# Notes on one change to an attention and squared-ReLU kernel: the first batch, the small first weights and two blocks of plain products

## The chip, the cores and the metric

The kernel runs on one core of one Trainium2 chip. The metric is the device time of one execution, in microseconds (us), as the median of several runs. The engines are TensorE (PE in the profile), VectorE (DVE), ScalarE (ACT), GpSimd (POOL) and SyncE (SP), which here only issues DMA transfers. Each engine takes its instructions in the order of the program; between engines they wait on semaphores.

## The reference

```python
def mab(q, kv):
    s = scale * (q @ kv.transpose(0, 2, 1))
    s = s - s.max(-1, keepdims=True)
    a = np.exp(s)
    a /= a.sum(-1, keepdims=True) + 1e-09
    return a @ kv
h = mab(I, x)            # I: inducing, (32, 128); x: (4, 12480, 128)
y = mab(x, h)            # (4, 12480, 128)
u = np.maximum(y.reshape(49920, 128) @ w_in, 0.0)    # w_in: (128, 2048)
out = u * u @ w_out                                  # w_out: (2048, 128)
```

For each of the four batches, 32 inducing rows attend to the 12480 rows of x (first attention) and give h, 32 rows. Then each row of x attends to these 32 rows (second attention), and its result goes through a feed-forward layer with a squared ReLU. The weights come as 64-bit floats.

## The kernel before, in words

**Blocks and groups.** The rows of a batch are cut into 26 lanes of 480 rows; four lanes are a group (the seventh group has two). A lane is also a block of the feed-forward part: 104 blocks. The second attention's weights for a lane, `st` (128x480, the 32 weights four times below each other, as high and low parts), are multiplied with `hw` = h @ w_in. So for each block PE makes 16 products `h` (L769), ACT takes the ReLU (L776) and the square (L790), DVE splits the squares into a high part (`hi`, L795) and a low part (`lo`, L800), and PE multiplies these with the split w_out: hi by wo_hi, hi by wo_lo, lo by wo_hi (L835), 45 products, and one of the 16 pieces in fp32 with `wo_whole` (L825), which PE does in two passes. The result bank `op` is turned by DVE (L855) and stored (L861).

**The first attention of batch 0** (class `First`, `early`): for each group in turn the rows `xn` come in one transfer (L407), PE turns them by transposes (L445) into `xtp`, ACT and DVE copy these out to `xt` (L242), PE makes the scores `sp` (L503), and then the group finds its maximum over rows and lanes (`mx`, `lanes`, `gather`, `most`, `neg`: L510 to L528), takes the exponentials `e` with that shift (L538), turns them to `et` (L548), mixes them with the rows (`nb`, L556), and adds that to what the groups so far gave, rescaled by `fade` (L566, L572). `first_end` then makes `zp`, `htp`, `hT` and, with w_in, the four pieces `wp` of `hw` (L623 to L632). The later batches' first attention runs between the blocks of the batch before, with rows turned on DVE: `xb` comes in 8 small transfers (L477) into the only such buffer, and DVE turns it (L480).

**Weights.** Each of the 8 pieces of w_in (i0 to i3) and w_out (o0 to o3) is loaded as words (L341, L353), sized on ACT and rebuilt on DVE in five steps, and joined; pieces of w_out are then split. The pieces share the buffers `hi` and `lo`, two each, with the blocks.

**Second attention** (class `Second`): scores `na` (L665), turned on DVE, maximum, difference, exponential on ACT, sum, normalised, turned back, split into `sw`, and spread by DMA to `st` (L713; 4 transfers for a lane, on SP's queue). For block 0 there is a small one of its own (`mini`, names with m: `na_0m`, `d_0m`, `sw_0m`), of four pieces of 128 rows, spread by 16 transfers on ACT's queue.

**What sets the order.** Nothing is issued as it is written. Each piece of work is a `Task` with an engine, a length, a due time and needs, and `Plan.run` places them one after another by these lengths and due times; in the order of that plan the instructions are then written out. The needs and due times set only the order on each engine. What an instruction waits for on the chip is its data and its buffers.

## Time and profile before

| | us |
|---|---|
| median of 3 runs | 1669.66 (1668.59 to 1670.12) |
| the profiled execution, own time | 1670.68 |
| its span | 1668.8 |
| PE busy in the span | 1617.4 (97%) |
| DVE busy | 1561.5 (94%) |
| ACT busy | 1522.7 (91%) |
| first `h` of block 0 starts | 81.44 |
| output turns of block 0, block 1 start | 111.50, 126.97 |

Rows of a timeline read: start, length, engine, line, operation, out<-in, shapes, count, and in brackets the engine's idle time ahead of it and what ended it. SPq and ACTq are the queues' issues of transfers. Rows of busy time by stretch read: stretch, its length, then PE, PEld, DVE, ACT and POOL busy with their counts, the clock granted to PE (1.00 is full), the busy share of the DMA engines, and GB/s. Rows of groups end with total busy time, mean ns of one, and idle time ahead.

### The profile page before, as it was taken

The numbers are of one execution on the slowest core, as the hardware profiler recorded it, in microseconds if no ns is written. First come the engines' busy times: TensorE is split into PE (matmuls) and PEld (weight loads), VectorE is DVE, ScalarE is ACT, GpSimd is POOL, SyncE is SP. The second block draws the span as 40 slices with busy tenths as digits, with TensorE's granted clock in tenths as the row PEclk, the third lists the DMA queues.
The fourth block names the chain that finished last, engine by engine and source line by source line (L and its number), as shares of the span: only waits on it lengthen the run. The fifth ranks groups of instructions, "written<-read, shape, count | busy, mean of one in ns | idle before, by whom it ended". The sixth has DMA issues, their size and how long they took to land.

```text
span 1668.8 us, 22357 instructions
## 1 busy us (share of the span) xinstructions
PE 1617.4 (97%) x8042; PEld 1289.8 (77%) x8042; DVE 1561.5 (94%) x1524; ACT 1522.7 (91%) x1444; POOL 49.0 (3%) x38
## 2 busy tenths in 40 slices
PE   7489999999999999999999999989999999999998
PEld 4168788887777888888877888877887788778886
DVE  7689999999999999999999999989999999989997
ACT  4289999999999999999989999989999999999997
POOL 0000000000001000000000000000000000000000
PEclk9689999999999999999999999999999999999999
DMA  7334333223243431334124433132111121111111
GB/s 248 84 68 94 64 75 81 41 55 72 47 89 60 86 79 31 74 53 88 30 58 93 82 59 78 36 66 54 24 30 40 39 42 36 36 35 35 21 28 20
DMA packets 389855, 101.57 MB, mean 61 GB/s; under 512 B 369232, under 2 KB 385904, under 8 KB 389744
## 3 DMA queue, kind: packets, MB, share of 16 engines
q1 hardware_dynamic: 388976, 99.89, 28.7%
q8 instruction: 64, 1.05, 0.3%
q14 instruction: 47, 0.39, 0.1%
q10 hardware_dynamic: 768, 0.25, 0.1%
HBM read 48.94 MB, written 25.56 MB: 45 GB/s over the span
## 4 chain that ended last, share of the span: by engine, by line
PE 91%; DVE 3%; DMA 2%; SPq 1%; ACT 1%; issue 1%; ACTq 0%; DVEq 0%
PE op L835 59%; PE h L769 21%; PE op L825 5%; PE na L665 1%; PE nb L556 1%; PE sp L503 1%; PE wp L623 1%; DVE lo L800 1%; SPq L477 1%; DMA st<-sw 0%; PE xtp L445 0%; ACT g L776 0%; ACT g L790 0%; DVE hi L795 0%; SPq L713 0%
## 5 line engine op out<-in xcount | busy, mean ns | idle before, releaser
L776 ACT ACTIVATE g<-h 128x960 f32<-128x960 f32 x832 | 781.2, 983 | 80.6 <-PE h L769 48.3
L800 DVE TENSOR_TENSOR lo<-g,hi 128x1920 fp32r<-128x1920 f32 (+2 forms) x419 | 839.9, 2005 | 12.6
L790 ACT ACTIVATE g<-g 128x1920 f32<-128x1920 f32 (+1 forms) x419 | 760.3, 1814 | 4.3
L769 PE MATMUL h<-st,hw 128*128 128x480 f32 x1664 | 510.9, 389 | 19.6 <-DMA xb<-in_x_dram 15.2
L795 DVE CAST hi<-g 128x1920 fp32r<-128x1920 f32 (+2 forms) x419 | 451.9, 1079 | 38.8 <-ACT g L790 33.9
L835 PE MATMUL op<-hi,wo_hi 128*128 128x480 f32 x1560 | 454.8, 405 | 0.5 <-DVE hi L795 0.4
L835 PE MATMUL op<-hi,wo_lo 128*128 128x480 f32 x1560 | 442.1, 382 | 0.0
L835 PE MATMUL op<-lo,wo_hi 128*128 128x480 f32 x1560 | 425.1, 382 | 6.4 <-DVE lo L800 6.4
L769 PEld LDWEIGHTS h<-st,hw 128*128 128x128 f32 x1664 | 310.7, 189 | 105.2 <-issue 38.0
L835 PEld LDWEIGHTS op<-hi,wo_hi 128*128 128x128 f32 x1560 | 293.1, 189 | 83.6 <-issue 37.4
L835 PEld LDWEIGHTS op<-lo,wo_hi 128*128 128x128 f32 x1560 | 291.5, 188 | 60.7 <-DVE lo L800 9.0
L835 PEld LDWEIGHTS op<-hi,wo_lo 128*128 128x128 f32 x1560 | 293.1, 188 | 49.2 <-issue 2.6
L825 PE MATMUL op<-g,wo_whole 128*128 128x480 f32 x208 | 100.5, 564 | 0.0
L690 POOL TENSOR_SCALAR z<-z 128x15 f32<-128x15 f32 (+1 forms) x28 | 47.9, 1711 | 1516.7 <-DVE z L686 1462.8
L855 DVE STREAM_TRANSPOSE ob<-op 128x480 f32<-128x480 f32 (+1 forms) x105 | 70.4, 671 | 4.1 <-PE op L835 3.9
L480 DVE STREAM_TRANSPOSE xt<-xb 128x960 f32<-128x960 f32 x39 | 45.3, 1163 | 7.5 <-DMA xb<-in_x_dram 5.3
L825 PEld LDWEIGHTS op<-g,wo_whole 128*128 128x128 f32 x208 | 38.9, 188 | 5.9
L556 PE MATMUL nb<-xn,et 128*32 128x128 f32 (+1 forms) x840 | 30.8, 280 | 5.8 <-DVE et L548 5.7
L556 PEld LDWEIGHTS nb<-xn,et 128*32 128x32 f32 (+1 forms) x840 | 23.5, 111 | 16.5 <-DVE et L548 9.4
L503 PE MATMUL sp<-xt,indT 128*32 128x480 f32 x208 | 31.2, 594 | 4.2 <-DVE xt L242 2.7
L242 ACT COPY xt<-xtp 128x256 f32<-128x256 f32 (+1 forms) x33 | 11.1, 366 | 21.1 <-PE xtp L445 17.9
L665 PE MATMUL na<-xt,hT 128*32 128x480 f32 (+1 forms) x224 | 27.5, 568 | 0.0
(103 smaller groups left out, 423.0 us busy)
## 6 DMA issues: line engine op xcount, KB each, us to landing
out_dram<-ob SPq DMA_DIRECT2D x412, 60.0 KB, 2.2
xn<-in_x_dram SPq DMA_DIRECT2D x24, 960.0 KB, 5.5
st<-sw SPq DMA_DIRECT2D x380, 60.0 KB, 2.0
xb<-in_x_dram SPq DMA_DIRECT2D x312, 60.0 KB, 2.6
xn<-in_x_dram SPq DMA_DIRECT2D x4, 480.0 KB, 4.9
hi_i<-in_moe_w_in_dram SPq DMA_DIRECT2D x2, 512.0 KB, 10.4
lo_i<-in_moe_w_in_dram SPq DMA_DIRECT2D x2, 512.0 KB, 8.5
hi_o<-in_moe_w_out_dram SPq DMA_DIRECT2D x2, 512.0 KB, 7.6
```

The lines of the kernel that those rows point to most:

```text
L480: nc.vector.transpose(self.xt_tile(h).rearrange("c l r t -> c (l r t)"), v["xb"].rearrange("p l r c -> p (l r c)"))
L503: nc.tensor.matmul(v["sp"][q * M:(q + 1) * M, :LANE], indT, s["xt"][self.g, q // 2][:, q % 2].rearrange("c r t -> c (r t)"), start=True, s ...
L556: nc.tensor.matmul(v["nb"][c * M:(c + 1) * M, :], self.et[:R, r, :], self.xn[:R, r, :], start=r < Q, stop=r >= NR - Q,)
L690: E.tensor_scalar(v["z"], v["z"], 1e-9, 0.0, ALU.add, ALU.add)
L769: nc.tensor.matmul(c["hp"][:, l, :LANE], s["hw"][:, f * P:(f + 1) * P], second.st[k], start=True, stop=True,)
L776: nc.scalar.activation(v["g"][:, 2 * i:2 * i + 2, :], c["hp"][:, :, :LANE], AF.Relu)
L790: nc.scalar.activation(v["g"][:, h], v["g"][:, h], AF.Square)
L795: nc.vector.tensor_copy(v["hi"][:, h], v["g"][:, h])
L800: nc.vector.tensor_sub(v["lo"][:, h], v["g"][:, h], v["hi"][:, h])
L825: nc.tensor.matmul(w["op"][:, :LANE], wo_whole, v["g"][:, 3, :], start=False, stop=False)
L835: nc.tensor.matmul(w["op"][:, :LANE], wo[:, 4 * j + l, :], v[name][:, l, :], start=(j == x_ == 0 and l == 0), stop=(j == NQ - 1 and x_ == ...
L855: nc.vector.transpose(w["ob"][:, rows].rearrange("p r c -> p (r c)"), w["op"][:, rows.start * S:rows.stop * S])
```

## The change

**First batch.** A class `FirstBatch` takes the place of seven early `First`. All groups are turned and scored first; the scores stay (groups 0 to 3 are copied to `sk` in `st` buffers, the last three stay in their PSUM banks), each group's maximum goes to a column of `bare`, and one maximum over all of them gives one `neg`. Then come seven exponentials, and all mixes accumulate in the one bank `nb`; there is no rescaling. Transposes fill two banks at once, so that an eviction is 8 or 7 row blocks of all four lanes (up to 1024 columns). x loads stand ahead of most weight loads on SP's queue. PSUM is given out anew when `hT` is done (`open_g`).

**Small first weights.** `mini` now takes four pieces that lie next to each other; DVE writes high and low parts side by side (`sk`), four PE products with an identity turn and repeat them into one bank (`ap`), and ACT and DVE copy that bank to `st`. The 16 transfers are gone.

**Blocks 0 and 1** (`PLAIN`): the squares are not split; 16 products with the joined fp32 pieces `whole` of w_out make a block. The pieces' split to wo_hi and wo_lo is done later, before block 2.

**Order.** Due times and lengths in the plan are changed (`T_MAIN`, `ORDER`, `W_DUE`, transfers, products); some tasks have added needs (`GATES`, `begun`, "spread", "products", "h"), which act on the order only. `xt` is one tile for each group instead of two.

```diff
-    GB, HB, LB, OB, MB, STB, XTB, XNB, XBB = 3, 2, 2, 2, 2, 6, 14, 2, 1
-    T_MAIN, BLOCK = 44100.0, 15100.0
-    ORDER = "x0 x1 i0 x2 i1 x3 i2 x4 i3 x5 x6 o0 o1 o2 o3".split()
-    W_DUE = [11900.0, 21000.0, 24900.0, 30200.0, 40500.0, 46000.0, 50000.0, 53300.0]
-    SPARE = (3, 5, 6)
-    FIRST_DUE, FIRST_STEP = 6000.0, 4300.0
+    GB, HB, LB, OB, MB, STB, XTB, XNB, XBB = 3, 2, 2, 2, 2, 6, 7, 2, 1
+    T_MAIN, BLOCK = 42100.0, 15100.0
+    ORDER = "x0 x1 x2 x3 i0 x4 x5 x6 i1 i2 i3 o0 o1 o2 o3".split()
+    W_DUE = [11900.0, 21100.0, 24900.0, 30200.0, 41500.0, 46000.0, 50000.0, 53300.0]
+    FIRST_DUE, FIRST_STEP, MIX_DUE, MIX_STEP, MINI_DUE = 6000.0, 2600.0, 25000.0, -1000.0, -800.0
     S2_LEAD, S2_LEAD_0, S2_STEP, S1_LEAD, S1_STEP = 44500.0, 26000.0, 1600.0, 11100.0, 3000.0
     WHOLE = lambda b, g, k: True
+    PLAIN = lambda b, g, k: b == g == 0 and k < 2
+    GATES = lambda s, m: dict(
+        s0=m.ready[0], s1=m.ready[0], s2=m.ready[0], s3=m.ready[0], w0_1=m.normed, w0_2=m.normed, w0_3=m.normed,
+        o1=m.normed, o2=m.normed, o3=m.normed,
+    )
+    SPLIT_DUE, SPLIT_STEP, PLAIN_DUE = 64000.0, 0.0, 9500.0
...
+    ps_t = early_scope.enter_context(tc.tile_pool(name="ps_t", bufs=2, space=PSUM))
+    ps_s = early_scope.enter_context(tc.tile_pool(name="ps_s", bufs=4, space=PSUM))
+    plan = Plan(dict(xn=XNB, early=5, tp=2, s=4, xb=XBB, xt=XTB, st=STB, m=MB, h=2, o=OB, g=GB, hi=HB, lo=LB, sw=1, a=1, d=2, e=2, et=2), T_MAIN, patience=PATIENCE)
...
-        pools["early_scope"].close()
+        early_scope.close()
+        pools["h"] = ctx.enter_context(tc.tile_pool(name="ps_h", bufs=2, space=PSUM))
+        pools["o"] = ctx.enter_context(tc.tile_pool(name="ps_o", bufs=OB, space=PSUM))
+        pools["m"] = ctx.enter_context(tc.tile_pool(name="ps_m", bufs=MB, space=PSUM))
+        wo_pool = ctx.enter_context(tc.tile_pool(name="wo", bufs=1, side="right"))
+        pools["wo"] = [wo_pool.tile([P, NF, C], F32R, name=f"wo_{part}") for part in ("hi", "lo")]
         pools["g"] = ctx.enter_context(tc.tile_pool(name="g", bufs=GB, side="right"))

...
             def use(v, needs, due, kw, k=k):
-                hi = wo_hi[:, k * m:(k + 1) * m, :].rearrange("p f c -> p (f c)")
-                lo = wo_lo[:, k * m:(k + 1) * m, :].rearrange("p f c -> p (f c)")
+                def part(i):
+                    return pools["wo"][i][:, k * m:(k + 1) * m, :].rearrange("p f c -> p (f c)")
+
+                def join():
+                    v["whole"] = v["a"].bitcast(F32)
+                    nc.vector.tensor_add(v["whole"], v["whole"], v["b"])
+
+                def keep():
+                    nc.scalar.copy(wo_whole, v["whole"][:, (m - 1) * C:m * C])

                 def split():
-                    nc.scalar.copy(hi, v["a"].bitcast(F32))
+                    nc.scalar.copy(part(0), v["whole"])

                 def rest():
-                    a = v["a"].bitcast(F32)
-                    on(tr).tensor_sub(a, a, hi)
-
-                def join():
-                    on(tj).tensor_add(lo, v["a"].bitcast(F32), v["b"])
-
-                def whole():
-                    c = slice((m - 1) * C, m * C)
-                    nc.vector.tensor_add(wo_whole, v["a"][:, c].bitcast(F32), v["b"][:, c])
-
-                t = add("ACT", 530, split, due, needs, **kw)
+                    nc.vector.tensor_sub(part(1), v["whole"], part(0))
+
+                t = add("DVE", 600, join, due, needs, port=True, **kw)
                 if k == n - 1:
-                    t = add("DVE", 200, whole, due, [t] + needs, port=True, **kw)
-                tr = add("DVE", length("DVE"), rest, due, [t], port=True, **kw)
-                tj = add("DVE", length("DVE"), join, due, [tr], port=True, **kw)
-                return tj
+                    w_kept.append(add("ACT", 280, keep, SPLIT_DUE, [t], **kw))
+                d = SPLIT_DUE + k * SPLIT_STEP
+                th = w_gate[f"s{k}"] = add("ACT", 530, split, d, [t], **kw)
+                tl = add("DVE", 600, rest, d, [th], port=True, **kw)
...
+    class FirstBatch:
...
+            t = add("DVE", 100, lanes, d - 3000, self.tops)
+            t = add("DVE", 110, lanes2, d - 3000, [t])
+            t = add("PE", 110, gather, d - 3000, [t], reads=[bg])
+            t = add("DVE", 100, most, d - 3000, [t], reads=[bg])
+            shifted = add("DVE", 70, shift, d - 3000, [t])
...
+            powered, mixed = None, None
+            for g in range(NG):
+                R = M * lanes_of[g]
+                c = {}
+                be, bet = Buffer("e"), Buffer("et")
+
+                def power(g=g, R=R, c=c):
+                    c["e"] = att.tile([P, NR, S], F32, tag="e", name=f"e_0_{g}")
+                    nc.scalar.activation(
+                        c["e"][:R].rearrange("p r t -> p (r t)"), self.sp[g], AF.Exp,
+                        bias=self.neg[:R], scale=scale, accum_out=bare[:R, 1, g:g + 1],
+                    )
...
+                def mix(g=g, R=R, c=c):
+                    if g == 0:
+                        v["nb"] = early_bank("nb_0")[:, :C]
+                    for r in range(NR):
+                        k = r % Q
+                        nc.tensor.matmul(
+                            v["nb"][k * M:(k + 1) * M, :], c["et"][:R, r, :], self.xn[g][:R, r, :],
+                            start=g == 0 and r < Q, stop=g == NG - 1 and r >= NR - Q,
+                        )
...
+                bank_ = Buffer("tp")
+                v = {}
+
+                def turn(rs=rs, v=v):
+                    v["tp"] = ps_t.tile([P, 8, P], F32, tag="tp", name=f"xtp_0_{g}_{rs.start}")
+                    for j, r in enumerate(rs):
+                        nc.tensor.transpose(v["tp"][:, j, :R], self.xn[g][:R, r, :], ident[:R, :R])
+
+                def turned(rs=rs, v=v):
+                    if rs.start == 0:
+                        s["xt"][g] = xt_pool.tile([C, Q, NR, S], F32, tag="xt", name=f"xt_0_{g}")
+                    copy(
+                        v["task"], s["xt"][g][:, :L, rs.start:rs.stop, :].rearrange("c l r t -> c r l t"),
+                        v["tp"][:, :len(rs), :R].rearrange("c r (l t) -> c r l t", l=L),
+                    )
+
+                t = state["turn"] = add(
+                    "PE", 109 * len(rs), turn, due + 300 * k / 4, [self.loaded[-1], state.get("turn")], mode="t",
+                    takes=[bank_], reads=[self.bxs[g]],
+                )
+                n = R * len(rs)
+                v["task"] = add("ACT|DVE", (wide_ns(n, "ACT"), wide_ns(n)), turned, due + 600 + 300 * k / 4, [t],
...
+
+            def keep():
+                self.sp[g] = st_pool.tile([P, LANE], F32R, tag="st", name=f"sk_0_{g}").bitcast(F32)[:R]
+                copy(c["keep"], self.sp[g], c["sp"][:R, :LANE])
+
+            t = add("PE", 950, score, due + 1200, turned_, mode="n", takes=[bs], reads=[bt])
+            self.tops.append(add("DVE", wide_ns(LANE), top, due + 2000, [t], reads=[bs]))
...
+            def high1():
+                v["sk"] = att.tile([P, NB, 2, 2, M], F32R, tag="sk", name=f"sk_{n}", bufs=1)
+                nc.vector.tensor_copy(
+                    v["sk"][:, :, :, 0, :], v["d"].rearrange("p r (o m) -> p r o m", o=1).broadcast_to([P, NB, 2, M])
+                )
+
+            def low1():
+                nc.vector.tensor_sub(
+                    v["sk"][:, :, :, 1, :], v["d"].rearrange("p r (o m) -> p r o m", o=1).broadcast_to([P, NB, 2, M]),
+                    v["sk"][:, :, :, 0, :],
+                )
+
+            def back1():
+                v["ap"] = bank(f"ap_{n}").rearrange("p (r i t) -> p i r t", r=NB, i=L)
+                for r in range(NB):
+                    nc.tensor.matmul(
+                        v["ap"][:, :, r, :], v["sk"][:, r].rearrange("p j a m -> p (j a m)"), identr,
+                        start=r == 0, stop=r == NB - 1, skip_group_check=True,
+                    )
...
+            mini = not to
...
+            if mini:
+                bt = Buffer("m")
+                self.bst[0] = Buffer("st")
+                t = add("DVE", 210, high1, d + 6 * step, [t], port=True, reads=[bd])
+                t = add("DVE", 335, low1, d + 6 * step, [t], reads=[bd])
+                t = add("PE", 440, back1, d + 7 * step, [t], takes=[bt], mode="r")
+                t0 = add("ACT", 460, lambda: stacked(0), d + 8 * step, [t], takes=[self.bst[0]], reads=[bt])
+                self.ready[0] = add("DVE", 160, lambda: stacked(1), d + 8 * step, [t, t0], reads=[bt, self.bst[0]])
+                return
...
+            if plain:
...
+                    for l in range(h.start, h.stop):
+                        def product(l=l):
+                            if j == l == 0:
+                                w["op"] = pools["o"].tile([P, 512], F32, tag="o", name=f"op_{n}")
+                            nc.tensor.matmul(
+                                w["op"][:, :LANE], wv["whole"][:, l * C:(l + 1) * C], v["g"][:, l, :],
+                                start=j == l == 0, stop=j == NQ - 1 and l == 3,
+                            )
+
+                        begin = j == l == 0
+                        last = add("PE", 810, product, due + PLAIN_DUE + 810 * l, [sq, last, w_whole],
+                                   takes=[bo] if begin else [], reads=[bg, wbuf] + ([] if begin else [bo]))
+                return last
```

PE around the first `h` (`sp` scores, `nb` mix, `zp` and `htp` sums and join, `na_0m` and `ap` of the small weights, `wp` products for `hw`). Before:

```order
L556 MATMUL nb_5_624<-xn_5_374,et_5_618 32x128 x15
L517 MATMUL sp_6_613<-lanes_6_643,same_m 128x2
L556 MATMUL nb_6_672<-xn_6_499,et_6_667 32x128 x15
L595 MATMUL zp_689<-zs_6_669,same_m 128x1
L610 MATMUL htp_707<-join_700,hacc_6_693 128x128
```

And now:

```order
L696 MATMUL sp_6_344<-xt_6_322,indT 32x480 x2
L577 MATMUL sp_6_344<-lanes_357,same_m 128x4
L619 MATMUL nb_377<-xn_0_121,et_0_373 32x128 x15
L619 MATMUL nb_377<-xn_1_123,et_1_395 32x128 x15
L619 MATMUL nb_377<-xn_2_125,et_2_417 32x128 x15
L619 MATMUL nb_377<-xn_3_147,et_3_437 32x128 x15
L619 MATMUL nb_377<-xn_4_188,et_4_457 32x128 x15
L619 MATMUL nb_377<-xn_5_218,et_5_479 32x128 x15
L725 MATMUL zp_503<-zs_500,same_m 128x1
L619 MATMUL nb_377<-xn_6_240,et_6_498 32x128 x15
L740 MATMUL htp_531<-join_526,hacc_528 128x128
L796 MATMUL na_0m<-xt_0_144,hT_533 32x128 x4
```

The gather of the maximum stands once, behind the last scores, and all mixes behind it; before, each group's gather and mix stood between the scores of later groups.

PE in blocks 0 and 1 now (`op_0_0` is block 0's result, `h_0_1_..` are block 1's first products, `sp_0`, `nb_0` with numbers from 746 on belong to batch 1):

```order
L984 MATMUL op_0_0_641<-g_0_0_2_672,hi_o_397 128x480
L465 MATMUL sp_0_746<-xt_0_669,indT 32x480 x4
L942 MATMUL h_0_1_0_755<-st_0_1_704,hw_535 128x480 x2
L942 MATMUL h_0_1_1_760<-st_0_1_704,hw_535 128x480 x2
L984 MATMUL op_0_0_641<-g_0_0_2_672,hi_o_397 128x480 x2
L479 MATMUL sp_0_746<-lanes_0_769,same_m 128x4
L942 MATMUL h_0_1_2_777<-st_0_1_704,hw_535 128x480 x2
L984 MATMUL op_0_0_641<-g_0_0_2_672,hi_o_397 128x480
L984 MATMUL op_0_0_641<-g_0_0_3_700,lo_o_459 128x480
L942 MATMUL h_0_1_3_794<-st_0_1_704,hw_535 128x480 x2
L984 MATMUL op_0_0_641<-g_0_0_3_700,lo_o_459 128x480 x2
L518 MATMUL nb_0_818<-xn_0_614,et_0_811 32x128 x15
```

SP's queue for the same stretch, now:

```order
L440 DMA xb_0_0_627<-in_x_dram 32x15x32 x8
L411 DMA xn_1_651<-in_x_dram 128x1920
L440 DMA xb_0_1_679<-in_x_dram 32x15x32 x8
L843 DMA st_0_1_704<-sw_0_693 32x480 x4
L843 DMA st_0_2_714<-sw_0_693 32x480 x4
L843 DMA st_0_3_722<-sw_0_693 32x480 x4
L440 DMA xb_1_0_737<-in_x_dram 32x15x32 x8
L440 DMA xb_1_1_799<-in_x_dram 32x15x32 x8
```

Batch 1's first scores and its first mix were behind block 1 before; now they stand in block 0, with their xb loads and the st transfers of blocks 1 to 3 in one queue.

SP's queue about two thirds through (batch 2's second attention, batch 3's xb), before:

```order
L861 DMA out_dram<-ob_3_0_9872 480x1x32 x4
L713 DMA st_4_0_9944<-sw_4_9923 32x480 x4
L713 DMA st_4_1_9955<-sw_4_9923 32x480 x4
L713 DMA st_4_2_9966<-sw_4_9923 32x480 x4
L713 DMA st_4_3_9979<-sw_4_9923 32x480 x4
L477 DMA xb_5_0_9989<-in_x_dram 32x15x32 x8
L861 DMA out_dram<-ob_3_1_10011 480x1x32 x4
```

And now:

```order
L440 DMA xb_4_1_9547<-in_x_dram 32x15x32 x8
L843 DMA st_4_0_9624<-sw_4_9607 32x480 x4
L843 DMA st_4_1_9632<-sw_4_9607 32x480 x4
L843 DMA st_4_2_9642<-sw_4_9607 32x480 x4
L843 DMA st_4_3_9658<-sw_4_9607 32x480 x4
L1054 DMA out_dram<-ob_3_0_9663 480x1x32 x4
L440 DMA xb_5_0_9706<-in_x_dram 32x15x32 x8
```

The transfers are the same; on DVE the turn of `xb_4_1` stands ten rows ahead of the turn of `xb_5_0` before, and 24 rows ahead of it now.

More of the change, by code (lines that the diff above doesn't have):

```diff
@@ L344, in join @@
                 def join():
-                    on(t).tensor_add(w_in_sb[:, sl], v["a"].bitcast(F32), v["b"])
-                t = add("DVE", length("DVE"), join, due, needs, port=True, **kw)
+                    nc.vector.tensor_add(w_in_sb[:, sl], v["a"].bitcast(F32), v["b"])
+                t = add("DVE", 600, join, due, needs, port=True, **kw)
                 return t
@@ L411, in __init__ @@
             self.loaded = state["load"] = add(
-                "SP", 750 * self.L if early else 2000, load,
-                ORDER.index(f"x{g}") * 10.0 - 1000.0 if early else due - 30000,
-                [state.get("load")] if not early else [], takes=[self.bx], late=0,
+                "SP", 2000, load, due - 30000, [state.get("load"), begun], takes=[self.bx], late=0,
             )
-            self.bt = [Buffer("xt") for _ in range(self.L // 2)]
+            s["bxt"][g] = self.bt = Buffer("xt")
@@ L480, in turn, with weigh @@
                 nc.vector.transpose(
-                    self.xt_tile(h).rearrange("c l r t -> c (l r t)"), v["xb"].rearrange("p l r c -> p (l r c)")
+                    self.xt_tile()[:, 2 * h:2 * h + 2].rearrange("c l r t -> c (l r t)"),
+                    v["xb"].rearrange("p l r c -> p (l r c)"),
                 )
-            t = state["blocks"] = add("SP", 2050, load, due - 20000, [state.get("blocks")], takes=[bb], late=0)
+            t = state["blocks"] = add("SP", 2050, load, due - 20000, [state.get("blocks"), self.begun], takes=[bb], late=0)
             t = state["turn"] = add("DVE", 1090, turn, due, [t, state.get("turn"), self.begun],
-                                    takes=[self.bt[h]], reads=[bb])
+                                    takes=[] if h else [self.bt], reads=[bb] + ([self.bt] if h else []))
             return t
-        def weigh(self, due, step, early):
+        def weigh(self, due, step):
             s, n, L, R = self.s, self.n, self.L, self.rows
@@ L752, in ffn_block @@
         part = BLOCK / NQ
-        last = None
+        last = state.get("products")
         def quad(j, last):
@@ L758, in quad @@
             bg, bhi, blo = Buffer("g"), Buffer("hi"), Buffer("lo")
-            exact = j == NQ - 1 and WHOLE(b, g, k)
+            plain = PLAIN(b, g, k)
+            exact = j == NQ - 1 and WHOLE(b, g, k) and not plain
+            wv, wbuf, w_whole, w_split = w_outs[j]
             relus = []
@@ L847, in ffn_block @@
             last = quad(j, last)
+        state["products"] = last
         at = b * N + (first_lane[g] + k) * LANE
@@ L885, in induced_attention_then_squared_relu_ffn @@
     w_ins, w_outs = load_weights(W_DUE)
-    for g in range(NG):
-        First(0, g, FIRST_DUE + FIRST_STEP * g)
-    t_end = FIRST_DUE + FIRST_STEP * NG + 1500
+    FirstBatch(FIRST_DUE, FIRST_STEP, MIX_DUE, MIX_STEP)
+    t_end = MIX_DUE + MIX_STEP * NG + 1500
     first_end(0, t_end, 600)
     seconds = {}
-    mini = Second(
-        0, 0, [(0, 0, 0, 0), (0, 0, 0, 128), (0, 0, 0, 256), (0, 0, 0, LANE - 128)], 128,
-        {0: [(0, 0, 128, 0), (1, 0, 128, 128), (2, 0, 128, 256), (3, 512 - LANE, 128, 384)]}, t_end + 1200, 400.0, "m",
-    )
+    mini = Second(0, 0, [0, 128, 256, 384], 128, {}, t_end + MINI_DUE, 300.0, "m")
     seconds[0, 0, 0] = mini
-    g_open = [add("SP", 1, open_g, T_MAIN, [state[0]["first"].summed], late=-2500)]
     open_early()
+    for name, task in GATES(state[0], mini).items():
+        w_gate[name].needs.append(task)
     begun = None
```

275 lines of the change are left out of this document (167 added, 108 removed).

## The prediction

> **What bounds the kernel now.** I read the page first, then busy time by stretch, then PE's waits, then the chain of waits in order of time.
>
> ```profile
> span 1668.8 us, 22357 instructions
> PE 91%; DVE 3%; DMA 2%; SPq 1%; ACT 1%; issue 1%; ACTq 0%; DVEq 0%
> ```
> ```profile
> 50.00:60.00 10.00, 7.11 (x46) 3.52 (x46) 7.59 (x19) 1.46 (x3) 0.00 (x0) 0.50 0.31 111
> 70.00:80.00 10.00, 0.00 (x0) 0.00 (x0) 3.60 (x6) 0.00 (x0) 0.00 (x0) 0.50 0.28 52
> 80.00:90.00 10.00, 7.70 (x16) 4.65 (x16) 4.79 (x8) 7.38 (x9) 0.31 (x1) 0.51 0.14 22
> 160.00:500.00 340.00, 339.54 (x1699) 271.58 (x1699) 327.50 (x305) 323.48 (x301) 9.37 (x6) 1.00 0.33 65
> 1000.00:1500.00 500.00, 493.89 (x2342) 398.33 (x2340) 469.66 (x416) 471.33 (x429) 15.88 (x10) 0.99 0.21 43
> ```
> ```profile
> PE h L769 <- DMA xb<-in_x_dram: 15.2, 1, 15.2
> PE h L769 <- DMA st<-sw: 3.4, 1, 3.4
> ```
> From 160 us on PE is never free (339.54 of 340), so there only PE's work counts, and a stall counts in full. Before 100 us PE is not the bound, and twice it works at a granted clock of 0.50. So the end is: the moment by which blocks 0 and 1 are through PE, plus PE's work after it, plus PE's stalls after it. I work out these three.
>
> **First batch up to the common maximum.** In the first batch the change takes out six of seven running maxima with their rescaling; PE then runs transposes and scores back to back.
>
> ```profile
> 5.84 3.79 PE L445 MATMUL xtp<-ident,xn 128*128 128x128 f32 x15 [2.98 <-DMA xn<-in_x_dram]
> 28.24 1.09 PE L445 MATMUL xtp<-ident,xn 128*128 128x128 f32 x8
> 27.05 1.26 PE L503 MATMUL sp<-xt,indT 128*32 128x480 f32 x8 [0.61 <-DVE neg L528]
> 4.29 0.44 SPq L341 DMA_DIRECT2D hi_i<-in_moe_w_in_dram  x1
> 46.58 0.14 DVE L528 SCALAR_TENSOR_TENSOR neg<-top,neg 128x1 f32<-128x1 f32 x1
> 34.42 0.65 DVE L510 TENSOR_REDUCE mx<-sp 128x1 f32<-128x480 f32 x1
> ```
> ```profile
> hi_i<-in_moe_w_in_dram SPq DMA_DIRECT2D x1, 512.0 KB, 13.0
> ```
> ```profile
> L776 ACT ACTIVATE g<-h 128x960 f32<-128x960 f32 x832 | 781.2, 983 | 80.6 <-PE h L769 48.3
> ```
> The first x group is there at 5.8 us. The weight piece issued at 4.29 landed at 17.3, with three more x groups and two more pieces (4.5 MB) since 5.8: 2.5 us for an x group, 1.3 for a piece. Now five x groups and a half with one piece between follow, so the last lands at 5.8 + 5x2.5 + 1.3 + 1.25 = 20.9. PE needs longer: 15 slow transposes of group 0 (0.27 each, 4.0), five groups at 15x0.137 = 2.05, 1.4 for the half, scores 6x1.3 + 1.0, some 1.0 for the slow start: 5.8 + 4.0 + 10.3 + 1.4 + 8.8 + 1.0 = 31.3. The evictions, now 960 to 1024 columns, cost about a relu of that width (0.98) and run beside the next scores. From the last score to the common `neg` DVE does a maximum (0.65) and some ten small steps between weight steps: 3.3 us. `neg` stands at 34.6; before it stood at 46.6.
>
> **Exponentials, mixes, first weights.**
>
> ```profile
> 29.26 1.07 PE L556 MATMUL nb<-xn,et 128*32 128x128 f32 x30
> 50.61 1.92 PE L556 MATMUL nb<-xn,et 64*32 64x128 f32 x30 [4.78 <-DVE et L548]
> 55.65 0.29 DVE L242 COPY hT<-htp 128x128 f32<-128x128 f32 x1 [0.28 <-PE htp L610]
> 58.79 0.32 DVE L672 STREAM_TRANSPOSE d_0m<-na_0m 128x128 f32<-128x128 f32 x1 [1.18 <-PE na_0m L665]
> 68.78 10.34 ACTq L713 DMA_DIRECT2D st<-sw_0m  x16
> 81.44 1.94 PE L769 MATMUL h<-st,hw 128*128 128x480 f32 x4 [15.25 <-DMA xb<-in_x_dram]
> ```
> PE idles some 5 us between its last score and the first mix; the mix after such a gap (4.78) took 1.92 instead of 1.07. The first transposed exponentials come 2.4 us after `neg`, at 37.0. Seven mixes at 1.07 end at 44.5, seven at 1.92 at 50.4; I take some 2.5 slow ones, 46.7. By the Trainium skill, "TensorE: Matmul & The Clock Gate", Part 1, the clock falls after an idle window of about 3.4 us and returns after a busy one: one or two slow mixes, an estimate of 46; the row of 1.92 agrees that the gap costs.
>
> Copy, join and `hT` take 1.2: `hT` at 47.9, against 55.9. From there the old way took 25.5 us to the first h, 10.3 of them the 16 issues on ACT's queue and most of the rest small steps (0.2 to 0.3 each) that stood behind steps of 0.65 on DVE. The new way has no transfer: nine small steps, two splits, four products into a bank, two copies. Its own chain is some 4.6, and two hw steps, one na and one wp stand in it: 7.8, plus 1.3 for handovers. First h at **57**; bounds 54 (all warm, no handovers) and 62 (all at half clock). The new shapes (`sk`, `ap`) have no row; they are bounded by 0.2 and 0.7 each.
>
> **Blocks 0 and 1.**
>
> ```profile
> 109.22 0.22 PE op L835
> 105.79 0.81 PE op L825 x2
> 108.78 0.44 PE h L769 x2
> 126.97 0.68 DVE L855 STREAM_TRANSPOSE ob<-op 128x480 f32<-128x480 f32 x1
> ```
> ```profile
> 103.16 5.61 SPq L477 DMA_DIRECT2D xb<-in_x_dram  x8
> 114.96 10.55 SPq L713 DMA_DIRECT2D st<-sw  x16
> 98.76 0.68 PE L769 MATMUL h<-st,hw 128*128 128x480 f32 x2 [3.35 <-DMA st<-sw]
> 100.00:102.00 2.00, 2.00 (x7) 1.65 (x6) 0.14 (x1) 2.00 (x2) 0.00 (x0) 0.50 0.30 73
> ```
> ```profile
> L480 DVE STREAM_TRANSPOSE xt<-xb 128x960 f32<-128x960 f32 x39 | 45.3, 1163 | 7.5 <-DMA xb<-in_x_dram 5.3
> xb<-in_x_dram SPq DMA_DIRECT2D x312, 60.0 KB, 2.6
> st<-sw SPq DMA_DIRECT2D x380, 60.0 KB, 2.0
> ```
> Two old blocks are 90 products at 0.22 and two at 0.81, 21.4 us; two plain ones are 32 at 0.81, 25.9: 4.5 more for PE, while DVE loses its splits. But PE alone doesn't set this stretch. The order puts a score of batch 1 ahead of block 1's first h, and a mix of batch 1 into block 0; these hang on the xb loads, which take turns in one buffer, each eight issues (5.3), 2.6 to land, 1.1 to turn, and share SP's queue with the st transfers. Relu, square and one exponential on ACT, then six DVE steps, end the first turn at 57 + 10.6 = 67.6. Then: second xb 67.6 + 5.3 + 2.6 + 1.1 = 76.6, which frees the score; twelve st issues (7.1) run on SP from 72.9 to 80.0; the next xb 80.0 + 5.3 + 2.6 + 1.1 = 89.0; row sum and transpose of `et`, behind that turn on DVE, 90.2; mix, slow, 92.1. PE then has 17 plain products (13.8) and ten pairs of h (4.4) to the end of block 1: 110.3, and some 2.5 for a half clock, as after the gap of 3.35 us at 98.76: 112.8. Before, block 1 was through at 126.8, ahead of its output transpose: **-14.0**. Without the SP chain PE's 39 us and 3 of waiting for ACT would end at 99, -27.8; a first h at 62 would make it -9.
>
> By the Trainium skill, "DMA: Bandwidth & Descriptors", Issuing engines are not separate DMA queues, initiating a DMA is usually short beside the DMA. The rows say otherwise for these small ones: 5.61 to issue, 2.6 to land. By the page the stretch would end near the 99.
>
> **What comes after.** The same 1620 h, 4590 split products and 102 whole ones follow in both programs. By the order the first batch's five score instructions and 15 mix instructions of batch 1 are now done earlier, and four second scores later: -1.25 - 1.07 + 1.0 = **-1.3**.
>
> ```profile
> 1112.96 1.18 DVE L480 STREAM_TRANSPOSE xt<-xb 128x960 f32<-128x960 f32 x1 [5.34 <-DMA xb<-in_x_dram]
> 1115.74 1.17 PE L835 MATMUL op<-lo,wo_hi 128*128 128x480 f32 x2 [4.26 <-DVE lo L800]
> 1120.67 1.04 PE L835 MATMUL op<-hi,wo_lo 128*128 128x480 f32 x4
> ```
> This late stall comes of one turn standing on DVE some 11 us behind the one that frees its buffer, with st issues and the load between. It costs 4.3, and half of the 4.6 until products run at 0.22 again: 6.6. In the new order no turn follows another with st issues between so closely: **-6.6**. What the new order adds: twice a turn with 7.1 us of DVE work since the last (7.9 needed; 0.7 in all), and at the start of batches 1 and 2 a store, an xb and a st on SP before the first h (2.6 + 5.3 + 2.4 + 2.0 = 12.3, against some 11 us of PE's work): 1 each. Together **+2.7**, between 0 and 8.
>
> Sum against the profiled execution's own 1670.7 (span 1668.8 and 1.9 around it): -14.0 - 1.3 - 6.6 + 2.7 = -19.2, 1651.5. The median of the runs is 1.0 lower: **1651**.
>
> **Rivals.** (1) SP's chain does not hold blocks 0 and 1 (a mix can come later than PE reaches it only if the loads are as slow as in the rows): end of block 1 near 100, 13 less, 1638. For it, DVE is nearly empty there and may turn earlier; against it, the 5.61 and the 15.2 us that PE once waited. (2) The start gains, but the moved order has a stall of its own as large as the late one: 6.6 more, 1658. The old plan had one in some 39 turns. (3) Slower: PE's clock. While block 0 is paced by ACT, PE has gaps; if they keep it at 0.50 through both plain blocks, 32 products take 1.62 and 22 pairs of h 0.88: 25.9 + 9.7 more, of which some 10 fall into the waits above: 25 more, 1676. It decides when PE's busy share there stays as in 80 to 90 us (7.70 of 10 at 0.51). Against it, the clock was back by 104 after the gap at 98. (4) The change doesn't get its early start: the fp32 products wait for the joined w_out pieces, the last of which stands behind the second turn on DVE (77.3 by my chain). Only if these came 12 us later would block 1 end where it did; with the late stall kept too, 1668.
>
> **Chances.** Forecast 0.58; (1) 0.15; (2) 0.18; (3) 0.05; (4) 0.04. Range 1639 to 1662: it takes in nearly all of (2) and the upper edge of (1), and the first h from 54 to 62. A measurement can tell 0.2%, 3.3 us, from no change: faster 0.91, same 0.04, slower 0.05.
>
> **What would show it.** `neg` of the first batch near 35, the first h near 57, without a transfer ahead of it; a wait of PE on an xt turn near 73 to 77 and on `et` near 85 to 90; the output transpose of block 1 near 113; no wait of 4 us in the 1000s. I am wrong if the first h comes after 65, if block 1 ends after 120, or if PE's busy time after block 1 shows new gaps of over 8 us in all.

## The result and the profile after

The changed kernel takes 1653.16 us (median of four runs, 1650.44 to 1654.28), against 1669.16 us before: the ratio is 0.9901, with a 95% interval from 0.9884 to 0.9918. The forecast was 1651. The profiled execution took 1653.15 us itself.

The page of the changed kernel, its span and its chain of waits by engine; then the places at which PE waited (total, times, longest):

```profile
span 1651.4 us, 22141 instructions
...
PE 89%; DVE 5%; SPq 2%; issue 2%; DMA 1%; ACT 1%; DVEq 0%; POOL 0%; ACTq 0%
```
```profile
PE nb L518 <- DVE et L510: 5.7, 1, 5.7
...
PE sp L465 <- DVE xt L443: 2.2, 1, 2.2
...
PE h L942 <- DMA st<-sw: 5.1, 2, 2.8
PE op L1027 <- DVE lo L973: 0.6, 2, 0.4
```

In the chain PE's share is 89% (91% before) and DVE's 5% (3%): what holds PE up is now more often DVE. The 15.2 us that PE waited ahead of the first h are gone, and so is the late stall on `lo` (PE's waits on `lo` were 6.4 in all before, 4.3 of them this stall, and are 0.6 now). Two new waits stand in blocks 0 and 1, and two on `st` at the starts of batches 1 and 2.

The timeline of the changed kernel (start, length, engine) has the landmarks of the prediction:

```profile
31.72 0.14 DVE L585 TENSOR_SCALAR neg<-top 128x1 f32<-128x1 f32 x1
...
44.74 0.29 DVE L254 COPY hT<-htp 128x128 f32<-128x128 f32 x1
...
53.97 0.70 PE L942 MATMUL h<-st,hw 128*128 128x480 f32 x2
...
63.03 5.24 SPq L440 DMA_DIRECT2D xb<-in_x_dram  x8
68.38 7.54 SPq L843 DMA_DIRECT2D st<-sw  x12
...
70.46 1.18 DVE L443 STREAM_TRANSPOSE xt<-xb 128x960 f32<-128x960 f32 x1 [2.85 <-DMA st<-sw]
...
76.02 15.50 SPq L440 DMA_DIRECT2D xb<-in_x_dram  x16
...
84.72 1.18 DVE L443 STREAM_TRANSPOSE xt<-xb 128x960 f32<-128x960 f32 x1 [6.73 <-DMA xb<-in_x_dram]
...
86.36 0.67 DVE L510 STREAM_TRANSPOSE et<-e 128x480 f32<-128x480 f32 x1
...
87.08 1.93 PE L518 MATMUL nb<-xn,et 128*32 128x128 f32 x30 [5.75 <-DVE et L510]
...
107.98 0.68 DVE L1048 STREAM_TRANSPOSE ob<-op 128x480 f32<-128x480 f32 x1
...
1644.89 0.75 DVE L1048 STREAM_TRANSPOSE ob<-op 128x256 f32<-128x256 f32 x2 [2.06 <-PE op L1027]
```

| | before | forecast | after |
|---|---|---|---|
| common `neg` ready | 46.7 | 34.6 | 31.9 |
| `hT` ready | 55.9 | 47.9 | 45.0 |
| first h starts | 81.4 | 57 (54 to 62) | 54.0 |
| second xt turn of batch 1 ends | | 76.6 | 71.6 |
| third ends | | 89.0 | 85.9 |
| first mix of batch 1 ends | | 92.1 | 89.0 |
| output turn of block 1 starts | 127.0 | about 113 | 108.0 |

So blocks 0 and 1 are through 19.0 us earlier. At the end 17.4 are left, since the last output turn of the kernel before stands here:

```profile
1662.32 0.75 DVE L855 STREAM_TRANSPOSE ob<-op 128x256 f32<-128x256 f32 x2 [1.99 <-PE op L835]
```

From block 1's output turn to the last one it is 1535.4 us before and 1536.9 after. The start gained 5 us more than forecast; the rest lost 1.6, where the forecast had a gain of 5.2. The experiments are about these two halves.

### The profile page after: what moved, and what is told of

Read it like the earlier page. It is cut to its first block, busy times and chain, and to the rows that moved or that the text cites. A ratio compares the mean times of both kernels' runs of the same rounds, so it can differ in the third digit from the quotient of the medians.

```text
span 1651.4 us, 22141 instructions
## 1 busy us (share of the span) xinstructions
PE 1615.4 (98%) x8004; PEld 1282.1 (78%) x8004; DVE 1535.6 (93%) x1457; ACT 1526.3 (92%) x1425; POOL 45.1 (3%) x39
## 4 chain that ended last, share of the span: by engine, by line
PE 89%; DVE 5%; SPq 2%; issue 2%; DMA 1%; ACT 1%; DVEq 0%; POOL 0%; ACTq 0%
PE op L1027 57%; PE h L942 21%; PE op L1017 5%; DVE lo L973 2%; SPq L440 1%; PE nb L518 1%; PE na L796 1%; DVE hi L968 1%; PE sp L465 1%; PE op L984 1%; PE xtp L671 1%; SPq L843 1%; PE wp L753 1%; DVE hw L762 0%; DMA st<-sw 0%
## 5 line engine op out<-in xcount | busy, mean ns | idle before, releaser
L973 DVE TENSOR_TENSOR lo<-g,hi 128x1920 fp32r<-128x1920 f32 (+1 forms) x409 | 823.7, 2015 | 15.2 <-DVE z L823 0.3
L968 DVE CAST hi<-g 128x1920 fp32r<-128x1920 f32 (+1 forms) x409 | 442.6, 1082 | 47.7 <-ACT g L963 39.7
L1027 PE MATMUL op<-hi,wo_hi 128*128 128x480 f32 x1530 | 442.5, 403 | 0.0
L1027 PE MATMUL op<-hi,wo_lo 128*128 128x480 f32 x1530 | 435.7, 383 | 0.0
L1027 PE MATMUL op<-lo,wo_hi 128*128 128x480 f32 x1530 | 415.4, 381 | 0.6 <-DVE lo L973 0.6
L1027 PEld LDWEIGHTS op<-hi,wo_hi 128*128 128x128 f32 x1530 | 286.2, 188 | 81.4 <-issue 36.6
L518 PE MATMUL nb<-xn,et 128*32 128x128 f32 (+1 forms) x630 | 23.4, 282 | 5.7 <-DVE et L510 5.7
L518 PEld LDWEIGHTS nb<-xn,et 128*32 128x32 f32 (+1 forms) x630 | 17.5, 112 | 13.0 <-DVE et L510 6.5
L465 PE MATMUL sp<-xt,indT 128*32 128x480 f32 x156 | 22.5, 578 | 2.2 <-DVE xt L443 2.2
L254 ACT CAST sw<-a 128x480 fp32r<-128x480 f32 (+1 forms) x25 | 14.2, 570 | 8.9 <-DVE a L830 8.8
## 6 DMA issues: line engine op xcount, KB each, us to landing
lo_i<-in_moe_w_in_dram SPq DMA_DIRECT2D x2, 512.0 KB, 17.4
```

What stands on the lines that cost most here:

```text
L518: nc.tensor.matmul(v["nb"][c * M:(c + 1) * M, :], self.et[:R, r, :], self.xn[:R, r, :], start=r < Q, stop=r >= NR - Q,)
L968: nc.vector.tensor_copy(v["hi"][:, h], v["g"][:, h])
L973: nc.vector.tensor_sub(v["lo"][:, h], v["g"][:, h], v["hi"][:, h])
L1027: nc.tensor.matmul(w["op"][:, :LANE], pools["wo"][wo][:, 4 * j + l, :], v[name][:, l, :], start=(j == x_ == 0 and l == 0), stop=(j == NQ - ...
```

## The experiments

All but e4 start from the changed kernel, with 1653.2 us as its time; each was run beside the kernel before, and the ratios are to that. The differences in microseconds are to the 1653.2, and each ratio's interval reaches some 2.3 us to either side; so a difference of under some 3 us says nothing by itself. They change the order of instructions by added needs in the plan, which put no wait on the chip; e6, e7 and e8 change more, as told there.

### e1: the exponentials ahead of the third turn

```diff
-            t = add("DVE", wide_ns(LANE), turn_e, due + 2.5 * step, [t], takes=[bet], reads=[be])
+            t = self.e_turned = add("DVE", wide_ns(LANE), turn_e, due + 2.5 * step, [t], takes=[bet], reads=[be])
...
+            if b == 0 and g == 0:
+                turned_e = state[1]["first"].e_turned
+            if b == 0 and g == 1:
+                state[1]["turned"][1][0].needs.append(turned_e)
```

> The changed kernel with one order moved: on DVE the row sum and the transpose of batch 1's first exponentials (et) stand ahead of the third xt turn, not behind it. Theory (queue of loads plus DVE's order): PE's wait of 5.75 us ahead of the mix at 87.08 is made by that turn, which waits for its load while et could go at about 80; so the wait falls below 1 us, the output transpose of block 1 comes at 101 to 102 instead of 107.98, and the time is 6 to 7 us under the changed kernel's 1653.2, about 1646.5. Rival (the exponential itself, or the gather of the maximum, is late): the wait stays above 4 us and the time within 1.5 us of 1653.2. Second rival (PE is then held by ACT's squares in block 1): wait gone, block 1 ends no more than 3 us earlier.

1644.83 us, ratio 0.9847 (0.9834 to 0.9861): 8.3 us less. The timeline of e1:

```profile
77.84 0.68 DVE L510 STREAM_TRANSPOSE et<-e 128x480 f32<-128x480 f32 x1 [0.23 <-ACT e L500]
...
79.99 1.07 PE L518 MATMUL nb<-xn,et 128*32 128x128 f32 x30
...
84.75 1.18 DVE L443 STREAM_TRANSPOSE xt<-xb 128x960 f32<-128x960 f32 x1 [6.10 <-DMA xb<-in_x_dram]
...
99.60 0.67 DVE L1048 STREAM_TRANSPOSE ob<-op 128x480 f32<-128x480 f32 x1
```

The turn waits for its load as before, until 84.75 instead of 84.72. But now nothing that PE needs stands behind it: `et` goes at 77.84 instead of 86.36, the mix has no wait and runs at 1.07 instead of 1.93, and block 1 ends 8.4 us earlier. Since e1's first h is 0.6 later (54.61), the stretch from there is 9.0 shorter. The wait is 5.75 of this, and the half clock behind it 1.3, as the expectation had it: from the mix to the output turn it takes 20.9 us in the changed kernel and 19.6 in e1. The last 2.0 lie ahead of that wait and are not the theory's. The earlier wait for the second turn is 0.3 shorter (1.91 and not 2.17), and behind it the changed kernel's profile shows 3.4 us at a clock of 0.50, e1's none (last section). So the load queue is late, but it is DVE's order that hands the delay to PE.

### e2: batch 1's first group later

```diff
-            First(b + 1, g, max(starts[b, g] - S1_LEAD, T_MAIN + 3000), begun if w == 0 else None)
+            First(b + 1, g, max(starts[b, g] - S1_LEAD, T_MAIN + (34000.0 if w == 0 else 3000)), begun if w == 0 else None)
```

> The changed kernel with batch 1's first group due 31 us later in the plan: its score and mix stand on PE behind block 1's h, the st transfers ahead of its second load. Theory: without the load chain blocks 0 and 1 are bound by PE (39 us) and some 3 us of waits for ACT from the first h at 54, so both waits (2.17 and 5.75) and the half clock behind them go, the output transpose of block 1 comes at 96 to 98 instead of 107.98; the score and mix of 2.1 us come back later, so the time is 8 to 9.5 us under 1653.2, about 1644.5. Rival (the plain products wait for the joined w_out pieces, the last joined at 72.2): block 1 ends no earlier than 103. Second rival: the moved score and mix wait for their own load in block 2, and half of the gain is given back there.

1655.35 us, ratio 0.9911 (0.9898 to 0.9925): 2 us more, which these runs can't tell from none, where 8 to 9.5 less were expected. Neither rival of that text names the place; the timeline of e2 does:

```profile
94.14 5.26 SPq L440 DMA_DIRECT2D xb<-in_x_dram  x8
...
101.51 1.18 DVE L443 STREAM_TRANSPOSE xt<-xb 128x960 f32<-128x960 f32 x1 [12.03 <-DMA st<-sw]
102.61 1.12 DVE L968 CAST hi<-g 128x1920 fp32r<-128x1920 f32 x1
...
103.79 1.17 PE L1027 MATMUL op<-hi,wo_hi 128*128 128x480 f32 x2 [9.63 <-DVE hi L968]
```

Blocks 0 and 1 did run without the two waits: PE's plain products were through at 94.2. But on DVE the fourth turn came ahead of `hi` of block 2. Its load was issued at 94.14, behind twelve st issues; the turn stood until 101.5, DVE did nothing for 12 us, and PE waited 9.63 us for the first split products. The whole gain went there. This run's theory reckoned with the queue and not with what stands behind the late turn on DVE.

### e3: st ahead of xb at the batch starts

```diff
+            hold = seconds[b, 0, 0].ready[0] if b and g == 1 else None
...
-            t = state["blocks"] = add("SP", 2050, load, due - 20000, [state.get("blocks"), self.begun], takes=[bb], late=0)
+            t = state["blocks"] = add("SP", 2050, load, due - 20000, [state.get("blocks"), self.begun, self.hold if h == 0 else None], takes=[bb], late=0)
```

(`hold` is handed to `First`, which keeps it as `self.hold`.)

> The changed kernel with the order of SP's queue changed at two places: at the start of batches 1 and 2 the four st transfers of the batch's first blocks stand ahead of one xb load instead of behind it. Theory: the waits of 2.77 us at 467.5 and 2.35 us at 868 are made by the eight issues of that load (5.3 us), and 2 to 3 us of half clock follow each; the waits go, and the time is 6.5 to 8 us under 1653.2, about 1646. Rival (only the wait counts, the clock behind it is hidden in the later order): 5 us less, 1648. Second rival (the xb load, now 10 us later, makes its turn on DVE wait, and the splits behind it): the wait moves to the lo products, and less than 2 us are gained.

In the changed kernel the start of batch 1 looks like this in the timeline:

```profile
455.40 2.61 SPq L1054 DMA_DIRECT2D out_dram<-ob  x4
458.19 5.27 SPq L440 DMA_DIRECT2D xb<-in_x_dram  x8
463.56 8.89 SPq L843 DMA_DIRECT2D st<-sw  x13
...
467.51 0.67 PE L942 MATMUL h<-st,hw 128*128 128x480 f32 x2 [2.77 <-DMA st<-sw]
```

e3 takes 1645.21 us, ratio 0.9853 (0.9839 to 0.9866): 8.0 us less, the upper end of what was expected. PE's waits of e3:

```profile
PE nb L518 <- DVE et L510: 5.3, 1, 5.3
...
PE h L942 <- DMA st<-sw: 0.2, 1, 0.2
```

The waits on st went from 5.1 to 0.2, and the wait of block 0 stayed. The two waits of 2.77 and 2.35 cost 4.5 and 2.5 us by the output turns around them. The first brought half clock with it (last section). Behind the second the changed kernel's clock stayed at 1.00, so the expectation's half clock holds for the first only. The last 1.0 of the 8.0 lies elsewhere, 0.7 of it already at block 1's output turn, and is within the noise.

### e4: the kernel before, without its late stall

```diff
+            if (b, g) == (2, 5):
+                seconds[2, 4, 0].ready[0].needs.append(state[3]["loads"][5, 0])
```

(`loads` keeps the load task of each turn.)

> The kernel before with one swap on SP's queue: the load of the xb whose turn ended in the late stall (1107.6 to 1113) stands ahead of the 16 st issues instead of behind them. Theory (prediction's term of 6.6 us): the wait of DVE (5.34) and of PE (4.26) and the half clock behind it go, the time is 5.5 to 6.6 us under 1669.2, about 1663, ratio 0.9963. Rival (the st transfers, now 5.3 us later, make PE wait for them): less than 2 us gained, with a wait of h on st.

1663.48 us, ratio 0.9958 (0.9946 to 0.9971): 6.7 us less than the 1670.18 of the same chip. Of PE's 6.4 us of waits on `lo` 2.7 are left:

```profile
PE op L836 <- DVE lo L801: 2.7, 3, 1.0
```

The prediction's 6.6 us for the late stall are what one swapped load is worth. It also means that 6.7 of the change's 16 us could be had without the change.

### e5: both order changes together

> The changed kernel with both order changes together: et ahead of the third xt turn on DVE, and at the starts of batches 1 and 2 the st transfers ahead of the xb load on SP's queue. Theory (two separate stalls, both of an in-order queue): the gains add, 8.3 and 8.0 us under 1653.2, so about 1637, ratio 0.980. Rival (the second stall gives back part of the first gain, since the plan's slack was used up): 1641 to 1645.

1637.36 us, ratio 0.9807 (0.9792 to 0.9821): 15.8 less than the changed kernel, with 16.3 as the sum of e1 and e3. The two stalls are separate.

### e6: small weights by DMA again

In `Second` the branch of the small weights is the old one: transpose back, split, and in place of `sk`, `ap` and the two copies

```diff
+            if mini:
+                self.bst[0] = Buffer("st")
+                self.ready[0] = add("ACT", 250, lambda: spread(0), d + 8 * step, [tl], late=0, takes=[self.bst[0]], reads=[bw])
+                return
```

> The changed kernel with the old way of block 0's small weights: transposed back, split, and spread by 16 transfers on ACT's queue in place of four products and two copies. Theory (prediction: the first h waits for these transfers, and the load chain of batch 1 starts with the first relu and moves with it): first h at 66 to 68 instead of 53.97, the output transpose of block 1 near 120 instead of 107.98, the time 11 to 13 us above 1653.2, near 1665. Rival (the load chain runs ahead of the first h, so that the waits of 2.2 and 5.8 us in blocks 0 and 1 shrink by what the h is later): the first h 13 later, block 1 only 5 to 6 later, near 1659.

1663.78 us, ratio 0.9964 (0.9951 to 0.9977): 10.6 more. The timeline of e6:

```profile
49.73 11.63 ACTq L843 DMA_DIRECT2D st<-sw_0m  x16
...
61.73 0.59 ACT L757 CAST hw<-wp 128x512 fp32r<-128x512 f32 x1 [13.75 <-DMA st<-sw_0m]
...
63.09 1.17 PE L939 MATMUL h<-st,hw 128*128 128x480 f32 x2 [10.28 <-DVE hw L762]
```

The first h comes at 63.1, 9.1 later, and block 1's output turn 9.5 later. The load chain moves with the first h, as the theory said (the wait on `et` is still 5.2); the first h itself was expected at 66 to 68. It waits less for the 16 transfers than for `hw`, whose copy stands behind their 11.63 us of issues on ACT.

### e7: no plain blocks

```diff
-    PLAIN = lambda b, g, k: b == g == 0 and k < 2
+    PLAIN = lambda b, g, k: False
```

> The changed kernel with blocks 0 and 1 split as all others (45 split products and one fp32 product each instead of 16 fp32 products), and w_out's split ahead of them; the later order is the planner's own and changes too. Theory: PE saves 4.5 us in the two blocks, but DVE gets 8 casts and 8 differences (26 us) into a stretch of 53 us in which it is busy for some 30, next to the turns that wait for loads; block 1 ends 3 to 10 us later, and the time is 1656 to 1663. Rival (PE's 4.5 us count, since the splits lie in DVE's free time): block 1 ends at 103 to 105, near 1649.

1662.22 us, ratio 0.9952 (0.9935 to 0.9968): 9.1 more. Only 1.5 of it are there at block 1's output turn (109.5). Busy times in blocks 0 and 1, first of e7, then of the changed kernel (stretch, length, PE, PEld, DVE, ACT, POOL):

```profile
50.00:110.00 60.00, 49.12 (x211) 32.60 (x212) 57.41 (x80) 42.60 (x47) 2.03 (x2) 0.86 0.40 91
```
```profile
50.00:107.00 57.00, 46.32 (x170) 23.85 (x170) 33.64 (x61) 41.46 (x45) 1.30 (x2) 0.94 0.42 93
```

With the splits DVE is busy 57.4 of 60 us: it becomes the bound, and PE's saving of 4.5 us isn't seen. In the stretch that they change the plain products are worth 1.5 us. The other 8 come later, in an order that the planner made anew. The first of PE's waits of e7 (0.6 in the changed kernel):

```profile
PE op L1027 <- DVE lo L973: 5.9, 6, 1.8
```

Of these 5.9 us 3.7 lie in blocks 0 and 1. Behind block 1's output turn PE waits 9.5 us in all, against 5.7 in the changed kernel, and is busy 4.3 us longer; half clock would do that, but no run separates it.

### e8: the loads on POOL's queue

```diff
-                        nc.sync.dma_start(v["xb"][c * S:(c + 1) * S, l], rows[c])
+                        nc.gpsimd.dma_start(v["xb"][c * S:(c + 1) * S, l], rows[c])
```

> The changed kernel with the xb loads issued by POOL instead of SP, in the same order on all other engines. Theory (what binds blocks 0 and 1 and the batch starts is that xb, st and stores share one queue that issues a transfer in 0.62 us): loads and st transfers overlap, the wait of 5.75 us shrinks to 1 or 2, the st waits of 2.77 and 2.35 us go, and the time is 12 to 16 us under 1653.2, near 1639. Rival (a transfer issued by POOL takes longer from start to landing, or its issue holds up DVE): the turns come later, and the time is above 1653.

1652.75 us, ratio 0.9899 (0.9884 to 0.9913): no difference that these runs can tell. Neither theory holds alone. Of e8 the issues with their time to landing, PE's waits, and the timeline:

```profile
xb<-in_x_dram POOLq DMA_DIRECT2D x312, 60.0 KB, 2.8
```
```profile
PE op L1027 <- DVE lo L973: 3.7, 4, 1.9
...
PE nb L518 <- DVE et L510: 2.1, 1, 2.1
```
```profile
1.58 5.43 POOL L440 DMA_DIRECT2D xb<-in_x_dram  x8 [0.18 <-issue]
...
28.98 0.66 ACT L287 ACTIVATE lo_i<-lo_i 128x512 f32<-128x512 f32 x1 [2.39 <-DMA lo_i<-in_moe_w_in_dram]
```

The mechanism was right: with a queue of its own the load is there earlier, the wait in block 0 falls from 5.75 to 2.06, and no wait on st is left. But on an empty queue the first load went out at 1.58 instead of 40, into the loads of x and the weights, and the first h came 4.4 later (58.4): ACT waited 2.39 us to size a weight piece, and evictions of x stood behind that. And POOL's own small step for the sums (`z`) now stands behind loads that wait for their buffer, which is where I place the new waits on `lo` (3.7); no run separates that. A transfer is hardly slower from POOL's queue: 2.8 us to land against 2.6.

### e9: e2 with hi ahead of the fourth turn, and st first

```diff
+                state.setdefault("hi", {})[b, g, k, j] = th
...
+            if b == 0 and g == 1:
+                state[1]["turned"][1][1].needs.append(state["hi"][0, 0, 2, 1])
```

> The late first group of e2 with the one thing changed that held it up there: the fourth xt turn, which waited for its load until 101.5 with hi of block 2 behind it on DVE, now stands behind hi and lo of block 2's first two quarters; the st transfers at the batch starts stand ahead as in e3. Theory (a turn that waits for its load holds up everything behind it on DVE, and this alone cost e2 its gain): PE's wait of 9.63 us on hi goes with some 2.5 us of half clock, and with the 8 us of e3 the time is 1655.4 - 12 - 8, near 1635, 2 us under the 1637.4 of e5. Rival (the queue itself is too slow: the turns come later still, and the first group's gather or mix waits for them): PE waits 4 us or more on lanes or et in block 2, and the time is 1639 or more.

1635.20 us, ratio 0.9793 (0.9779 to 0.9806): the fastest of all. In the timeline the turn that cost e2 its gain starts at the same moment:

```profile
101.52 1.18 DVE L443 STREAM_TRANSPOSE xt<-xb 128x960 f32<-128x960 f32 x1 [3.14 <-DMA st<-sw]
```
```profile
PE op L1028 <- DVE hi L968: 0.6, 1, 0.6
```

The load is as late as in e2 (101.52 against 101.51), and PE waits 0.6 instead of 9.63. This settles e2: its loss was the place of the turn on DVE, not the queue's pace.

### e10: the old order of the first loads

```diff
-    ORDER = "x0 x1 x2 x3 i0 x4 x5 x6 i1 i2 i3 o0 o1 o2 o3".split()
+    ORDER = "x0 x1 i0 x2 i1 x3 i2 x4 i3 x5 x6 o0 o1 o2 o3".split()
```

> The changed kernel with the old order of the first loads on SP's queue: a piece of w_in between every two x groups, so three more pieces of 512 KB ahead of the last x. Theory (prediction: x lands long before PE is through, and PE's transposes and scores set the common maximum): the last x comes some 4 us later, at about 25, the neg and the first h move by less than 1.5 us, the time stays within 1.5 us of 1653.2. Rival (the loads bind the first batch): the last score, neg and the first h come 3.5 to 4.5 us later, and the time is 1656.5 to 1658. Second rival (earlier weights help ACT and DVE, which wait for the pieces in their own order): up to 2 us faster.

1656.88 us, ratio 0.9919 (0.9906 to 0.9933): 3.7 more, the number of the first rival. The intervals of the two ratios overlap, but the profiles agree: the first h is 3.9 later (57.84) and the last output turn 4.1. The rival's reason is only a part of it. The timeline of e10:

```profile
24.88 1.06 PE L671 MATMUL xtp<-ident,xn 128*128 128x128 f32 x8 [1.13 <-DMA xn<-in_x_dram]
...
29.42 0.69 ACT L287 ACTIVATE hi_o<-hi_o 128x512 f32<-128x512 f32 x1 [2.42 <-DMA hi_o<-in_moe_w_out_dram]
...
31.99 1.59 PE L696 MATMUL sp<-xt,indT 128*32 128x480 f32 x4 [1.41 <-ACT xt L254]
```

PE waits 1.1 us for x once. The rest are evictions (2.7 us on ACT in all): ACT waited 2.42 us for a weight piece, to size it, and the eviction of the last group stood behind that. So the new load order is worth some 3.9 us of the 27.5 by which the first h comes earlier, and most of it through the order of ACT's instructions.

## Why the prediction was right, and where it was not

**What held.** PE is the bound behind the start, and the start is not bound by PE: both halves show in the rows. The first h was forecast at 57 with 54 as the lower bound and came at 53.97. The chain from the first h to the mix came link for link, 3 to 5 us earlier as the first h was: second turn 5.0 earlier than forecast, third turn 3.1, mix 3.1. SP's issues took 5.24 for eight and 7.54 for twelve, against 5.3 and 7.1. e1 and e9 show that this chain, together with DVE's order, set the end of block 1. Rival (1), that it doesn't, is out; with its waits taken away block 1 ends at 95 to 100, where that rival had put it. The term of the late stall, 6.6, measured 6.7 (e4). Rival (3), a cold clock through both plain blocks, is out: from 50 us on the clock was 0.50 in two stretches of some 3.4 us only, behind the waits of 2.17 and 5.75, and the first of them cost nothing, since PE then waited for `et` anyway. Rival (4) is out too: the last joined piece stood at 72.2, and in all of blocks 0 and 1 the plain products waited 0.2 us, for ACT's squares.

**Too pessimistic, by 5 us: the start.** Three of them are the first batch: its scores took 1.0 us for four lanes and not 1.3, so the last one ended at 28.6 instead of 31.3; from there to `neg` it was 3.3 as forecast, and `hT` and the first h kept the lead. Another 2.5 are the half clock that I added for products after the mix; some 0.6 went again, between block 1's last product and its output turn. Busy times and granted clock (the third number from the end) of the changed kernel:

```profile
88.00:90.00 2.00, 2.00 (x21) 1.44 (x14) 1.47 (x4) 0.00 (x0) 0.00 (x0) 0.52 0.50 79
90.00:92.00 2.00, 2.00 (x8) 1.09 (x7) 0.36 (x1) 1.07 (x2) 0.00 (x0) 1.00 0.54 85
```

The slow stretch ended with the mix and a product or two, and from the mix's end at 89.0 to the first product of block 2 at 107.1 it took just the 18.2 us of work. The first batch's own mixes ended at 43.4, 11.6 us behind `neg`. By my 2.5 slow mixes it would have been 12.1. The estimate by the Trainium skill, "TensorE: Matmul & The Clock Gate", Part 1, one or two slow mixes, would have been 11.4. The trace agrees with it: six mixes took 7.93 us where warm ones take 6.4, at a clock of 0.50 until 38.7.

**Too optimistic, by 7 us: what comes after.** The step that failed is "at the start of batches 1 and 2 ... 1 each". The chain was right: forecast 12.3 us from the output turn to st, and 455.4 to 467.5 in the rows of e3's section, 12.1. What I had wrong was PE's work beside it, 11 us by the forecast and 9.3 by the trace, and that half clock can follow such a wait. The two waits, 1 each in the forecast, measure 2.77 and 2.35, and some 7 us with the half clock; the term of +2.7 thus measures 7 to 8 (e3). This is what rival (2) describes, a stall of the new order as large as the late one; it came in two pieces, and the gain at the start hid it in the sum.

**A term that wasn't there.** Of the -1.3 for attention done earlier, 1.25 was a first score with its gather, and the score is some 1.0 of that. In the kernel before it already stood ahead of block 1's output turn at 126.97; only the gather and the mix stood behind it, not "first scores" as the section on the change has it:

```profile
123.65 1.01 PE L503 MATMUL sp<-xt,indT 128*32 128x480 f32 x8
```

The stretch behind block 1's output turn, in e4 and in e5, that is, before and after without the large late stalls:

```profile
125.30:1656.00 1530.70, 1526.89 (x7462) 1231.11 (x7460) 1467.13 (x1335) 1456.07 (x1335) 45.72 (x29) 1.00 0.28 55
```
```profile
99.20:1630.00 1530.80, 1529.40 (x7447) 1232.63 (x7445) 1469.48 (x1326) 1460.27 (x1340) 43.96 (x29) 1.00 0.29 55
```

Both hold 148 records of that score's kind. The two rests are equal to 0.1 us, but not alike: PE is busy 2.5 us longer in e5 and idle 2.4 us less, since e4 still waits 2.7 us for `lo`. Some 1.3 of the 2.5 are records (eight products more in this stretch, 1.7, and small differences in the attention, -0.4); the rest stays open.

**The queue rule.** "DMA: Bandwidth & Descriptors", Issuing engines are not separate DMA queues, of the Trainium skill takes the issue of a transfer to be usually small beside the transfer. For one transfer the trace agrees: 0.66 us to issue, 2.6 to land. What counts here is a group: eight issues follow one another and take 5.24 us, while their landings overlap (the turn starts 7.4 us after the first issue). The prediction set eight issues against one landing and so read a contradiction. e8 is the test of what follows: a second queue saved 3.7 of the 5.75 us of wait.

So the mechanism at the start was right and its size wrong, and the total came out within 2.2 us by luck: two errors of 5 and 7 us met.

## What to carry to other kernels

On engines that work in order, look for what stands behind an instruction that waits for a transfer: e1 gained 8.3 us, and e9 12 over e2 beside the 8 of e3, without making the late load come earlier. Count a queue of small transfers by its issues (0.63 to 0.66 us each in the rows of eight and twelve here), and put what the next stage waits for ahead of what only fills a buffer. In a kernel bound by one engine, price a stall at its length, and up to some 1.7 us more for half clock: the one of 5.75 us cost 7.1 (e1), the one of 2.77 cost 4.5 and the one of 2.35 cost 2.5 (e3).
